# Gated attention and a low-rank mixer on one core: the mixer's work in three places per batch instead of four

## The chip, the cores and the metric

The kernel runs on one core of a Trainium2 chip. Its time is the device time of one execution in microseconds (us). TensorE (PE) multiplies, ScalarE (ACT) and VectorE (DVE) work on the results, GpSimd (POOL) issues most of the transfers and SyncE (SP) issues the transposing ones. Each engine works through its own queue in the order in which the program wrote it, and waits at an instruction until its semaphores are there.

## The reference

Two blocks, one behind the other, for 8 batches of 3136 positions with 256 channels (z has 64):

```python
scores = (1.0 / S) * np.matmul(z, z.transpose(0, 2, 1))
attn = np.maximum(scores, 0.0) ** 2
x = u * np.matmul(attn, v)                 # gated attention

h = x.transpose(0, 2, 1) @ U @ V           # U: 3136 x 32, V: 32 x 3136
y = x + h.transpose(0, 2, 1)               # low-rank mixing of the positions
out = y + np.maximum(y @ w_ch1, 0.0) @ w_ch2   # 256 -> 1024 -> 256
```

The low-rank sums `x^T U` need all positions of a batch; so the second block of a batch can only start when its attention is done.

## The kernel before, in words

**Tiles.** A batch has 25 tiles of 128 positions, the last with 64 (`NF`). An "output" is one such tile of the attention's result. The outputs of a batch are made in the order 12, 13, ..., 24, 0, ..., 11; the loop counts them as i = 0 to 24 (`turns(i)`), and this text says "output i" with that count. Two outputs share a pair of PSUM banks (a "pair": 0 and 1, 2 and 3, ..., 10 and 11; output 12, the short tile, stands alone; then 13 and 14, and so on).

**Attention.** z is laid twice, on both halves of the 128 partitions, so that two matmuls of 64 rows run side by side in the array. The score matrix is symmetric, so `A[j]` holds 13 blocks of a row of tiles (`score`, L307 on TensorE, relu on ACT L320, square on DVE L322), and the other 12 blocks of an output come as a "strip": a DMA transpose of `A` (`turn`, L342) that SP issues four outputs ahead. Output i multiplies its 25 blocks with v (`half`, L420; `quarter`, L460, for the short tile). When a pair is complete, `close_pair` adds the two banks (ACT L434, DVE L435), multiplies with u and writes x (DVE L450). A pair that opens takes the set of banks that the pair before it did not use; the other set is the `spare()` one.

**Mixer.** The 25 outputs of a batch form seven chunks of 4, 4, 4, 3, 4, 4 and 2. `rank_once` (L534) makes the rank sums with 25 matmuls of 128 x 32; `low_rank` (matmuls L586, adds on DVE L600) adds the low-rank part to a chunk of x in place and has it transposed (`turn_x`, L559, SP). `up_steps` (L618, relu on ACT L636) and `down_steps` (L665) are the two layers. A down step of a pair ends in an add on DVE (L679) into one of two `o_sb` buffers and in a store that POOL issues (L692; L694 for the short tile). `low_rank` and the down steps use the spare banks.

**The order of the work is written by hand.** While batch b's attention runs, the mixer of batch b-1 is done in between. Behind output 0 come the rank sums of b-1. `ahead` puts `low_rank` of chunks 0 to 6 inside outputs 2, 3, 6, 7, 10, 11 and 14, at step 10, 12 or 17 of the 25. `bursts_of(b)` makes a list of eight mixer steps: step n is the up layer of chunk n merged with the down layer of chunk n-1 (step 0 has only up, step 7 only down). `burst_at` places them, two and two, behind outputs 4, 8, 13 and 17. The scores that later outputs and the next batch need are spread into the outputs (`own_at`, `next_at`, `_spread`). The next batch's v comes in nine loads (`V_PARTS`, L244 and L247), merged into the mixer steps; its z is loaded at output 1 (output 5 in batch 1), copied twice on DVE (`double_z`, L188) in a mixer step, and transposed by SP at outputs 7 and 10 (`turn_z`, L195). In the last batch the steps of chunk 6 wait in `late`, and behind the loop stands the mixer of the last batch.

**Where x lies.** `x_bf` has room for 32 tiles, as eight slots of four. Chunk c of batch b takes slot (7 b + c) mod 8. The weights `w_ch1` pass through slots 6 and 7 at the start.

Of the kernel before, what the change touches and what calls it, by code (L numbers as in the profile page):

```python
# [8 lines left out]
BF16 = mybir.dt.bfloat16  # L9
# [5 lines left out]
def _ceil_div(a, b):  # L15
    return (a + b - 1) // b
# [26 lines left out]
def kernel(  # L43
# [28 lines left out]
    FIRST = HALF  # L72
# [1 line left out]
    LEAD = FIRST + AHEAD  # L74
    NG = 4
    XR = 32
    XB = 28

    ctx.enter_context(
        tc.manual_schedule(engines={ENG.PE, ENG.SP, ENG.Pool, ENG.DVE, ENG.Activation})  # L80
# [1 line left out]
    persist = ctx.enter_context(tc.tile_pool(name="persist", bufs=1))  # L82
# [42 lines left out]

    v_both = [persist.tile([P, NT, D], BF16, name=f"v{k}") for k in range(2)]
    eye = persist.tile([P, P], BF16, name="eye")
    x_bf = persist.tile([P, XR // 4, 4 * D], BF16, name="x_bf")
    A = [persist.tile([P, NB * P], BF16, name=f"A{j}") for j in range(NT)]


# [3 lines left out]
    def place(t):  # L135
        return (t - FIRST) % NT
# [9 lines left out]
    chunks = [[0, 1, 2, 3], [4, 5, 6, 7], [8, 9, 10, 11], [12, 13, 14]]  # L146
    chunks += [[15, 16, 17, 18], [19, 20, 21, 22], [23, 24]]
    chunks = [[turns(i) for i in c] for c in chunks]
    widths = [sum(P if t < NF else TAIL for t in c) for c in chunks]
    NC = len(chunks)  # L150
    offset = {t: (n, k) for n, c in enumerate(chunks) for k, t in enumerate(c)}

    def group(b, c):
        n = len(chunks[c])
        flat = x_bf[:, ((XB // 4) * b + c) % (XR // 4), : n * D]
        return flat.rearrange("p (a t c) -> p a t c", a=ND, c=P)

    def x_at(b, t, n=1):
# [81 lines left out]
    def load_v(b, part):  # L240
        t0, t1 = part
        v_bf = v_both[b % 2]
        if t0 < NF:
            pool_dma(out=v_bf[:, t0:t1, :], in_=rows(v[b])[:, t0:t1, :])  # L244
        else:
            for r in halves:
                pool_dma(out=v_bf[r, NF, :], in_=v[b, NF * P :, :])  # L247

    V_PARTS = [(t, t + 3) for t in range(0, NF, 3)] + [(NF, NT)]
    WHOLE = ((0, NF),)  # L250

    def weight_steps():


        w1_tmp = x_bf[:, NC - 1 :, :].rearrange("p a h -> p (a h)")
        w1_tmp = w1_tmp[:, : ND * H].rearrange("p (a h) -> p a h", a=ND)

        def first_w():
            pool_dma(out=w1_tmp, in_=moe_w_ch1.rearrange("(t p) d -> p t d", p=P))

        def second_w():
            pool_dma(out=w2_bf, in_=moe_w_ch2.rearrange("(p t) d -> p t d", t=NH))

        def order_w(a):
            nc.vector.tensor_copy(
                out=w1_bf[:, a, :].rearrange("p (t q) -> p t q", q=P),
                in_=w1_tmp[:, a, :].rearrange("p (q t) -> p t q", t=NH),
            )
# [26 lines left out]
        orders = [lambda a=a: order_w(a) for a in range(ND)]  # L295
        return fetches, second_w, puts + [put_tail, copies] + orders
# [403 lines left out]
    def bursts_of(b):  # L700

        out_ = []
        for c in range(NC + 1):
            alone = c == 0 or (c == NC - 1 and b == B - 2)
            up = [lambda s=s, c=c, a=alone: up_steps(c, a)[s]() for s in range(NH // 2)]
            up = up if c < NC else []
            down = down_steps(b, c - 1) if c else []
            out_.append((up, down))
        return out_
# [183 lines left out]
    start_up()  # L893
    puts = dict(zip((13, 14, 15, 16, 17, 18, 19, 20), puts))
    late = []
    for b in range(B):
        more = b + 1 < B
        begin = 0 if b else 2 * NG
        bursts = bursts_of(b - 1) if b else []
        burst_at = {4: (0, 1), 8: (2, 3), 13: (4, 5), 17: (6, 7)}  # L900
        own = own_at if b else first_at
        v_at = dict(zip((14, 16, 18, 20, 22, 10), V_PARTS[3:]))
        ahead = dict(zip((2, 3, 6, 7, 10, 11, 14), range(NC)))
        for i in range(begin, NT):
            o = turns(i)
            fill = [s for key in own.get(i, ()) for s in score_steps(b, *key)]
            if b == 0 and i in first_new:
                fill += rebuild_steps(b, first_new[i])
            if b == 0 and i in first_more:
                fill.append(lambda pair=first_more[i]: make_stored(pair, LEAD + 2 * NG))  # L910
            if more:
                coming = next_at if b else after_first
                fill += [s for key in coming[i] for s in score_steps(b + 1, *key)]
                if b and i == (1 if b > 1 else 5):
                    load_z(b + 1, WHOLE)
                if b == 0 and i == 9:
                    double_z(b + 1, ((FIRST, NF), (0, FIRST)))
                if i == (7 if b > 1 else 11 - 2 * b):
                    turn_z(b + 1, ((FIRST, NF),))
                if i == (10 if b else 12):  # L920
                    turn_z(b + 1, ((0, FIRST),))
                if b == 0 and i in v_at:
                    load_v(b + 1, v_at[i])
                if i == (12 if b else 14):
                    extend_z(b + 1)
            main = attend_steps(b, o)
            if b and i in ahead:
                at = 17 if (i + (i > FIRST)) % 2 == 0 else 12 if i == 7 else 10
                main.insert(at, lambda c=ahead[i]: low_rank(b - 1, c))
            _spread(main, fill)  # L930
            if b == 0 and i in first_turns:
                for t in first_turns[i]:
                    turn(b, t)
            elif i + AHEAD < NT:
                turn(b, turns(i + AHEAD))
            elif more:
                turn(b + 1, turns(i + AHEAD - NT))
            elif i == NT - AHEAD:
                turn_x(b, 0)
            if b == 0 and i in puts:  # L940
                puts[i]()
            if (b, i) == ((1, 1) if more or b else (0, 20)):
                second_w()
            if b and i == 0:
                rank_once(b - 1, spare()[0])
            for n in burst_at.get(i, ()) if b else ():
                up, down = bursts[n]
                if not more and n >= NC - 1:
                    late += up + (down if n == NC else [])
                    up, down = [], (down if n < NC else [])  # L950

                steps = [down.pop(0)] if n == 4 else []
                steps += _merge(up, down)
                if more:
                    loads = [lambda k=k: load_v(b + 1, V_PARTS[k]) for k in ((n,) if n < NC else (n, n + 1))]
                    steps = _merge(steps, loads)
                    if n == (1 if b > 1 else 3):
                        for k, part in ((6, (FIRST, NF)), (3, (0, FIRST))):
                            steps.insert(k, lambda part=part: double_z(b + 1, (part,)))
                run(steps)  # L960
# [4 lines left out]
    b = B - 1  # L965
    last = bursts_of(b)
# [9 lines left out]
    for c in range(NC + 1):  # L976
        up, down = last[c]
        steps = _merge(up, down)
# [32 lines left out]
```

## Time and profile before

| | us |
|---|---|
| runs | 999.24, 994.98, 994.67 |
| median | 994.98 |
| profiled execution | 1000.6 |
| its span, first to last instruction | 998.9 |
| TensorE busy in it | 983.7 |
| ScalarE, VectorE, GpSimd busy | 614.8, 554.7, 170.3 |
| rank sums of batches 1 to 7 start at | 101.2, 222.95, 348.6, 469.58, 590.56, 713.58, 834.56 |

The page gives busy times by engine and by line. An answer by windows gives, for a stretch of the span, its length, the busy time of PE, PEld, DVE, ACT and POOL with the number of instructions, the granted TensorE clock (1.00 is full), the share of the DMA engines and GB/s. A line of the timeline has the start, the length, engine, line, operation, tiles (written<-read), the shape of the array and of the operand, and how many; a bracket holds the idle time before it and what ended it. Starts are measured; the end of a matmul is modelled, so neighbouring lines overlap. A line of waits has the waiting group, the group waited for, the sum in us, the number of times and the longest.

### The profile page before, as it was taken

To read this page: it belongs to the slowest core of one execution; us is meant where nothing else is said; L and a number is where in the kernel's file an instruction comes from. 1 tells how busy PE (TensorE), PEld (TensorE's weight loads), DVE (VectorE), ACT (ScalarE), POOL (GpSimd) and SP (SyncE) were. 2 spreads that over 40 slices of the span, in tenths; PEclk is the share of its full clock that TensorE was granted. 3 is DMA by queue.
4 is the path that set the end of the run, shared out by engine and by line. 5 is a ranking of instruction groups with operands and counts; after the bars stand their busy time and mean duration, and the time that the engine had idled before them with its cause. 6 is when DMAs were issued, how large, how long until landed. Compare 5 with 4: busy or idle time off the path is not lost.

```text
span 998.9 us, 31057 instructions
## 1 busy us (share of the span) xinstructions
PE 983.7 (98%) x13697; PEld 780.3 (78%) x13697; DVE 554.7 (56%) x1020; ACT 614.8 (62%) x845; POOL 170.3 (17%) x316
## 2 busy tenths in 40 slices
PE   8999999999998999999999999999999999999998
PEld 5778777887877878788787887778878788787866
DVE  6888654466544665456644566445664457542352
ACT  8978764577644776466754667556674666643154
POOL 5111112211111111221112211112111120011000
PEclk9999999999999999999999999999999999999999
DMA  9999989899899998999899997999979997679633
GB/s 197 167 181 196 196 161 203 174 171 170 168 165 165 172 170 173 180 177 172 158 178 178 182 168 148 187 167 182 170 149 194 173 185 157 124 149 163 129 93 104
DMA packets 410728, 167.17 MB, mean 167 GB/s; under 512 B 386320, under 2 KB 395216, under 8 KB 410592
## 3 DMA queue, kind: packets, MB, share of 16 engines
q1 hardware_dynamic: 382272, 98.90, 62.8%
q0 software_dynamic: 28320, 66.28, 28.8%
q8 instruction: 107, 1.75, 0.8%
q14 instruction: 29, 0.24, 0.1%
HBM read 61.88 MB, written 25.69 MB: 88 GB/s over the span
## 4 chain that ended last, share of the span: by engine, by line
PE 88%; DMA 5%; issue 3%; DVE 2%; ACT 1%; POOL 1%; DVEq 0%; POOLq 0%; ACTq 0%
PE ps L420 47%; PE ps L665 16%; PE ps L618 16%; PE ps L307 7%; DMA out_dram<-o_sb 3%; DMA strip<-A 1%; PE ps L586 1%; ACT A L320 1%; PE ps L460 1%; DVE A L322 1%; DMA zT<-z_bf 1%; PE ps L534 1%; DMA ut<-x_bf 1%; DVE both L435 0%; PE ps L207 0%
## 5 line engine op out<-in xcount | busy, mean ns | idle before, releaser
L320 ACT ACTIVATE A<-ps 128x832 bf16<-128x832 f32 (+9 forms) x481 | 359.2, 764 | 150.1 <-PE ps L307 143.9
L420 PE MATMUL ps<-v,A 64*128 64x256 bf16 x4988 | 342.3, 270 | 2.3 <-DVE A L322 1.1
L322 DVE TENSOR_TENSOR A<-A 128x832 bf16<-128x832 bf16 (+9 forms) x481 | 243.9, 523 | 127.3 <-ACT A L320 125.5
L420 PE MATMUL ps<-v,strip 64*128 64x256 bf16 x4420 | 308.2, 269 | 1.4 <-DMA strip<-A 1.4
L420 PEld LDWEIGHTS <-A 64*128 64x128 bf16 x4988 | 248.3, 94 | 45.3 <-issue 10.5
L636 ACT ACTIVATE relu_bf<-ps 128x1024 bf16<-128x1024 f32 (+2 forms) x206 | 186.3, 912 | 140.2 <-PE ps L618 140.2
L420 PEld LDWEIGHTS <-strip 64*128 64x128 bf16 x4420 | 224.8, 94 | 34.2 <-DMA strip<-A 2.3
L679 DVE TENSOR_TENSOR o_sb<-ps,x_bf 128x512 f32<-128x512 f32 (+2 forms) x105 | 69.9, 665 | 244.4 <-PE ps L665 214.2
L665 PE MATMUL ps<-w_bf,relu_bf 128*128 128x256 bf16 (+1 forms) x1600 | 201.2, 273 | 0.0
L618 PE MATMUL ps<-ut,w_bf 128*128 128x512 bf16 (+2 forms) x896 | 198.6, 353 | 0.4 <-DMA ut<-x_bf 0.4
L665 PEld LDWEIGHTS <-relu_bf 128*128 128x128 bf16 (+1 forms) x1600 | 152.9, 98 | 45.6 <-issue 3.6
L618 PEld LDWEIGHTS <-w_bf 128*128 128x128 bf16 x896 | 84.9, 98 | 62.5 <-issue 6.5
L404 POOL DMA_DIRECT2D u_sb<-in_u_dram x96 | 53.7, 560 | 462.9 <-DVE x_bf L450 440.6
L307 PE MATMUL ps<-zT 64*128 64x416 bf16 (+9 forms) x812 | 132.3, 313 | 0.1
L434 ACT COPY both<-ps 128x512 f32<-128x512 f32 (+1 forms) x104 | 58.9, 567 | 73.2 <-PE ps L420 67.1
L692 POOL DMA_DIRECT2D out_dram<-o_sb x84 | 45.9, 547 | 276.2 <-DVE o_sb L679 269.8
L435 DVE TENSOR_TENSOR both<-ps,both 128x512 f32<-128x512 f32 (+1 forms) x104 | 69.3, 666 | 28.6 <-ACT both L434 28.0
L600 DVE TENSOR_TENSOR x_bf<-ps,x_bf 128x512 bf16<-128x512 f32 (+1 forms) x112 | 65.5, 626 | 11.6 <-PE ps L586 11.3
L450 DVE TENSOR_TENSOR x_bf<-both,u_sb 128x512 bf16<-128x512 f32 (+1 forms) x104 | 69.8, 671 | 3.6
L307 PEld LDWEIGHTS <-zT 64*128 64x128 bf16 x812 | 43.5, 94 | 4.2 <-DMA zT<-z_bf 0.4
L244 POOL DMA_DIRECT2D v<-in_v_dram x61 | 34.1, 561 | 1.2 <-DMA z_c<-in_z_dram 0.8
L307 PE MATMUL ps<-relu_bf 64*128 64x416 bf16 (+9 forms) x117 | 23.1, 337 | 3.1 <-ACT A L320 2.2
(61 smaller groups left out, 212.9 us busy)
## 6 DMA issues: line engine op xcount, KB each, us to landing
u_sb<-in_u_dram POOLq DMA_DIRECT2D x96, 256.0 KB, 3.8
out_dram<-o_sb POOLq DMA_DIRECT2D x84, 256.0 KB, 3.3
v<-in_v_dram POOLq DMA_DIRECT2D x57, 192.0 KB, 4.7
strip<-A SPq DMA_TRANSPOSE x194, 5.4
out_dram<-o_sb SPq DMA_DIRECT2D x11, 256.0 KB, 2.0
z_c<-in_z_dram POOLq DMA_DIRECT2D x7, 384.0 KB, 5.9
u_sb<-in_u_dram POOLq DMA_DIRECT2D x16, 64.0 KB, 2.7
ut<-x_bf SPq DMA_TRANSPOSE x56, 3.7
```

The lines of the kernel that those rows point to most:

```text
L307: mm(out=ps[:, k, :n], lhsT=zT[halves[k], j, :], rhs=zT_flat[halves[k], c : c + n], start=True, stop=True,)
L320: nc.scalar.activation(out=dst, in_=src, func=AF.Relu, scale=sc)
L322: nc.vector.tensor_tensor(out=dst, in0=dst, in1=dst, op=ALU.mult)
L420: mm(out=acc[t0][h][:, (o - t0) * D : (o - t0 + 1) * D], lhsT=w[halves[h]], rhs=v_both[b % 2][halves[h], j, :], start=start, stop=stop, **kw,)
L434: nc.scalar.copy(out=both[:, :w], in_=banks[1][:, :w])
L435: nc.vector.tensor_tensor(out=both[:, :w], in0=banks[0][:, :w], in1=both[:, :w], op=ALU.add)
L450: nc.vector.tensor_tensor(out=x_at(b, t0, n), in0=split(both[:, :w]), in1=u_sb[:, :n, :].rearrange("p t (a c) -> p t a c", c=P), op=ALU.mult,)
L600: nc.vector.tensor_tensor(out=q, in0=split(ps[h][:, : len(ks) * D]), in1=q, op=ALU.add)
L618: mm(out=ps[i][:, :w] if apart else ps[:, i, :w], lhsT=w1_bf[:, db, (hp + i) * P : (hp + i + 1) * P], rhs=uT[c][:, db, len(chunks[c]) * P ...
L636: nc.scalar.activation(out=relus[c][:, hp : hp + 2, :w], in_=ps[:, :, :w], func=AF.Relu)
L665: mm(out=ps[r, k * D : (k + 1) * D], lhsT=relus[c][:, ht, q : q + (TAIL if two else P)], rhs=w2_bf[:, ht, :], start=(ht < 1 + two), stop=( ...
L679: nc.vector.tensor_tensor(out=o_sb[:p].rearrange("p t (a c) -> p t a c", c=P), in0=split(ps[:p, k0 * D : (k + 1) * D]), in1=x_at(b, t, nk) ...
```

## The change

The mixer steps of a batch are placed three times instead of four: steps 0, 1, 2 behind output 4, steps 3, 4, 5 behind output 10, and steps 6, 7 behind output 0 of the batch after the next, directly behind the rank sums of the next one. (The last batch keeps steps 6 and 7 of the batch before it behind output 17, as it was.) Batch 1 has no place behind output 0. `low_rank` moves to outputs 1, 2, 3, 6, 7, 9 and 14. The down sums of the short tile no longer open their place; they lie inside the run of three. Chunks 5 and 6 of x now live into the batch after the next, so the slots of four are gone: `place_groups` lists for each chunk when it is first written and last read, and finds each a place among the 32 tiles. v's nine loads go one into each mixer step, and what is left of them (one, or three in batch 1) to outputs 13, 15 and 17. In batch 1 z's copies stand at output 8, outside a mixer step.

```diff
-    XB = 28
...
+    def bursts_at(b):
+
+        at = {0: (NC - 1, NC)} if b > 1 else {}
+        if b:
+            at.update({4: (0, 1, 2), 10: (3, 4, 5)})
+        if b == B - 1:
+            at[17] = (NC - 1, NC)
+        return at
+
+    def place_groups():
+
+        items = []
+        for b in range(B):
+            for c, ts in enumerate(chunks):
+                begin = b * NT + place(ts[0]) + (0 if place(ts[0]) == FIRST else 1)
+                last = NT * B
+                for d in (1, 2):
+                    for i, ns in bursts_at(b + d).items() if b + d < B else ():
+                        if c + 1 in ns and (d == 1) == (i > 0) and not (b == B - 2 and c == NC - 1):
+                            last = (b + d) * NT + i
+                items.append((begin, last, len(ts), (b, c)))
+        items.sort()
...
+        return {items[k][3]: p for k, p in enumerate(at)}
+
+    spot = place_groups()
+
     def group(b, c):
         n = len(chunks[c])
-        flat = x_bf[:, ((XB // 4) * b + c) % (XR // 4), : n * D]
+        flat = x_bf[:, spot[b, c] * D : (spot[b, c] + n) * D]
...
-        bursts = bursts_of(b - 1) if b else []
-        burst_at = {4: (0, 1), 8: (2, 3), 13: (4, 5), 17: (6, 7)}
+        all_bursts.append(bursts_of(b))
+        burst_at = bursts_at(b)
+        v_in = list(V_PARTS) if more and b else []
...
-        ahead = dict(zip((2, 3, 6, 7, 10, 11, 14), range(NC)))
+        ahead = dict(zip((1, 2, 3, 6, 7, 9, 14), range(NC)))
...
-                if b == 0 and i == 9:
+                if b < 2 and i == (8 if b else 9):
                     double_z(b + 1, ((FIRST, NF), (0, FIRST)))
...
+                if i in (13, 15, 17) and v_in:
+                    load_v(b + 1, v_in.pop(0))
...
-            for n in burst_at.get(i, ()) if b else ():
-                up, down = bursts[n]
-                if not more and n >= NC - 1:
+            for n in burst_at.get(i, ()):
+                up, down = all_bursts[b - 1 if i else b - 2][n]
+                if i and not more and n >= NC - 1:
                     late += up + (down if n == NC else [])
                     up, down = [], (down if n < NC else [])
 
-                steps = [down.pop(0)] if n == 4 else []
+                steps = [down.pop(0)] if n == 4 and n == burst_at[i][0] else []
                 steps += _merge(up, down)
                 if more:
-                    loads = [lambda k=k: load_v(b + 1, V_PARTS[k]) for k in ((n,) if n < NC else (n, n + 1))]
-                    steps = _merge(steps, loads)
-                    if n == (1 if b > 1 else 3):
+                    steps = _merge(steps, [lambda part=part: load_v(b + 1, part) for part in [v_in.pop(0)]])
+                    if b > 1 and n == 1:
                         for k, part in ((6, (FIRST, NF)), (3, (0, FIRST))):
                             steps.insert(k, lambda part=part: double_z(b + 1, (part,)))
                 run(steps)
```

More of the change, by code (lines that the diff above doesn't have):

```diff
@@ L127 @@
     eye = persist.tile([P, P], BF16, name="eye")
-    x_bf = persist.tile([P, XR // 4, 4 * D], BF16, name="x_bf")
+    x_bf = persist.tile([P, XR * D], BF16, name="x_bf")
     A = [persist.tile([P, NB * P], BF16, name=f"A{j}") for j in range(NT)]
@@ L151, with put_in @@
     offset = {t: (n, k) for n, c in enumerate(chunks) for k, t in enumerate(c)}
+    def bursts_at(b):
[17 more added lines that the diff above has]
+        items.sort()
+        at = []
+        def put_in(k):
+            if k == len(items):
+                return True
+            begin, last, n, _ = items[k]
+            held = [
+                (at[m], at[m] + items[m][2]) for m in range(k) if items[m][1] >= begin
+            ]
+            for p in sorted({0} | {q1 for _, q1 in held} | {q0 - n for q0, _ in held}):
+                if 0 <= p <= XR - n and all(p + n <= q0 or q1 <= p for q0, q1 in held):
+                    at.append(p)
+                    if put_in(k + 1):
+                        return True
+                    at.pop()
+            return False
+        assert put_in(0)
+        return {items[k][3]: p for k, p in enumerate(at)}
+    spot = place_groups()
     def group(b, c):
         n = len(chunks[c])
-        flat = x_bf[:, ((XB // 4) * b + c) % (XR // 4), : n * D]
+        flat = x_bf[:, spot[b, c] * D : (spot[b, c] + n) * D]
         return flat.rearrange("p (a t c) -> p a t c", a=ND, c=P)
@@ L252, in weight_steps @@
     def weight_steps():
-        w1_tmp = x_bf[:, NC - 1 :, :].rearrange("p a h -> p (a h)")
-        w1_tmp = w1_tmp[:, : ND * H].rearrange("p (a h) -> p a h", a=ND)
+        w1_tmp = x_bf[:, (NT - 1) * D : (NT - 1) * D + ND * H].rearrange("p (a h) -> p a h", a=ND)
         def first_w():
@@ L895 @@
     late = []
+    all_bursts = []
     for b in range(B):
```

## The prediction

> **What bounds the kernel now.** I read the page's busy table, then the stages of one batch each, then who waited for whom, then the timeline around mixer places. "Output i" is the i-th attention output of a batch in loop order (0 to 24), a "place" a run of mixer steps behind an output.
>
> The busy table, and the same table cut at the rank sums (L534) of batches 1 to 7, one line per batch:
>
> ```profile
> PE 983.7 (98%) x13697; PEld 780.3 (78%) x13697; DVE 554.7 (56%) x1020; ACT 614.8 (62%) x845; POOL 170.3 (17%) x316
> ...
> 101.20:222.95 121.75, 121.22 (x1706) 96.32 (x1704) 67.07 (x122) 75.50 (x103) 22.46 (x42) 1.00 0.96 180
> 222.95:348.60 125.65, 122.83 (x1707) 98.67 (x1705) 67.14 (x122) 75.59 (x103) 21.76 (x41) 0.99 0.98 168
> 348.60:469.58 120.98, 120.98 (x1705) 96.39 (x1703) 67.08 (x122) 75.60 (x103) 21.73 (x41) 1.00 0.97 175
> 469.58:590.56 120.98, 120.98 (x1705) 96.39 (x1703) 66.98 (x122) 75.50 (x103) 21.73 (x41) 1.00 0.97 173
> 590.56:713.58 123.02, 121.35 (x1706) 98.17 (x1704) 66.69 (x122) 75.52 (x103) 21.73 (x41) 1.00 0.97 172
> 713.58:834.56 120.98, 120.98 (x1705) 96.39 (x1703) 67.08 (x122) 75.61 (x103) 21.75 (x41) 1.00 0.96 174
> ```
>
> TensorE is the bound. Three batches take 120.98 us to the hundredth, busy throughout: nothing else shows in them. The others take 0.77, 4.67 and 2.04 us more, 7.5 us together. The profiled execution took 1000.6 us (span 998.9 and 1.7 around it); without the 7.5 it would be 993.1. The median, 994.98, so still has about 1.9 us of such waits.
>
> Where they come from, in the waits (us in total, times, longest) and the chain behind the longest:
>
> ```profile
> DVE o_sb L679 <- DMA out_dram<-o_sb: 30.0, 8, 5.5
> ...
> PE ps L586 <- DVE o_sb L679: 3.5, 2, 2.8
> ...
> PE ps L420 <- DVE o_sb L679: 1.0, 1, 1.0
> ```
>
> ```profile
> 292.87 10.01 DMA out_dram<-o_sb
> ...
> 303.00 0.70 DVE o_sb L679
> 303.75 0.29 PE ps L586 x2
> ```
>
> There are two o_sb buffers, so the add of an output pair waits for the store of the pair two before it. Behind the place at output 13 a store took 10.01 us, the add sat on DVE, and `low_rank` at output 14, which needs the PSUM banks that this add reads, held TensorE. It happened again at 670.39. The third (1.0 us, at about 643) is the next pair's opening behind the place at output 8.
>
> What entering and leaving a place costs, on TensorE's timeline (start, length):
>
> ```profile
> 409.50 0.94 PE L420 MATMUL ps<-v,A 64*128 64x256 bf16 x14
> 410.27 0.19 PE L307 MATMUL ps<-zT 64*128 64x64 bf16 x2
> ...
> 412.21 0.27 PE L420 MATMUL ps<-v,A 64*128 64x256 bf16 x2
> 412.42 0.63 PE L665 MATMUL ps<-w_bf,relu_bf 128*64 128x256 bf16 x8
> ...
> 424.26 1.04 PE L665 MATMUL ps<-w_bf,relu_bf 128*128 128x256 bf16 x8
> 425.23 0.72 PE L420 MATMUL ps<-v,A 64*128 64x256 bf16 x10
> ```
>
> Seven pairs of half-array matmuls start in 0.77 us, 0.11 a pair; the last pair before L665 takes 0.21. Eight L665 matmuls take 0.87 (8 x 0.109, as everywhere in these runs of steps), yet L420 starts 0.97 after them. Each change of array shape (64\*128, 128\*128, 128\*64, 128\*32) costs 0.10 us.
>
> **The change, part by part.**
>
> *Shape changes.* Counted in the two built orders of matmuls: 121 before, 108 after, on the same 13697 matmuls. In a batch from 2 to 6: four places made 8, rank sums 2, output 12 (64\*64) 2, and one more because the place at 13 opened with the 128\*64 sums of the short tile: 13. After: 128\*32 goes straight into the mixer, so rank sums and place 0 make 3; two places 4; the 128\*64 sums now lie inside a place, 2; output 12 2: 11. That is 10 fewer over five batches, 3 fewer in batch 1 (no place at 0), none in batch 7. 13 x 0.10 = 1.3 us less, all on TensorE's path. The Trainium skill, "TensorEngine Tiling (Array Packing)", Key Properties, says that changing the tiling mode, not merely the tile, drains TensorE; it gives no time.
>
> *Places 13 and 17 go.* With 13 goes the wait of `low_rank` at output 14: the nearest place is then three outputs (some 8 us) back. In the profile these waits were worth 2.98 us (303.75 less 300.22 and five pairs) and 0.7 us idle and, behind the first, a slow clock:
>
> ```profile
> 303.70:307.30 3.60, 3.56 (x44) 3.04 (x45) 2.00 (x5) 2.15 (x3) 0.54 (x1) 0.69 0.39 110
> ```
>
> Granted clock 0.69; that batch's 4.67 is thus 2.98 idle and about 1.6 of slow clock. Together 5.3 us off the profile, and batch 1's 0.77 (a chunk transpose late for its place at 8, z's late at output 12) too, since both now have a place more of lead.
>
> *The place at 10 is three steps.* It stores six times (one of them the short tile). From steps in the trace (L665 x8 0.87, L618 x4 0.87 at 512 columns, 0.55 at 320): pairs end 2.8, 5.7, 7.2, 10.6, 15.0 and 18.5 us in. A store is issued 1.2 us after its pair ends (0.7 of it the add) and lands a median 3.3 later. The third add wants the first store at 7.2 against 2.8+1.2+3.3 = 7.3: DVE waits, TensorE not, because the bank of that add is next written at about 12.4. The first store may be some 8 us late before TensorE stops. The place at 4 stores four times, 3.5 us apart, and needs nothing new.
>
> *The place at 0.* It is the old place 17 moved: up of chunk 6, down of 5 and 6, three stores. But `low_rank` of chunk 0 now follows at output 1, step 10:
>
> ```profile
> 437.69 0.61 PE L618 MATMUL ps<-ut,w_bf 128*128 128x256 bf16 x4
> ...
> 444.78 0.39 PE L420 MATMUL ps<-v,A 64*128 64x256 bf16 x4
> ```
>
> ```profile
> 441.50 0.55 POOL L692 DMA_DIRECT2D out_dram<-o_sb  x1 [3.27 <-DVE o_sb L679]
> ...
> 444.88 0.69 DVE L679 TENSOR_TENSOR o_sb<-ps,x_bf 128x512 f32<-128x512 f32 x1 [1.05 <-PE ps L665]
> ```
>
> On this pattern the third add ends 445.57 and `low_rank` would come at 444.78+1.27 = 446.05 (ten steps and a score, as 355.88 to 357.15 in batch 3): 0.5 us to spare. The first store must land by 446.05-0.69-0.05 = 445.3, that is within 3.8 us. Medians at place 17 are 2.8 to 4.1, so I take 0.1 us a batch (0.6), with 0 below and, at 6.3, the median of the short tile's store (behind output 13), 2.5 us a batch above. The Trainium skill, "DMA: Bandwidth & Descriptors", Anatomy of one DMA, fits 2.0 us plus bytes over 436 kB per us: an estimate of 2.6 for 256 KB, by which this wait never comes; the trace's median is 3.3.
>
> *`low_rank` moves* from outputs 2,3,6,7,10,11,14 to 1,2,3,6,7,9,14. Its matmuls and adds are the same. At an odd output its DVE adds (2 x 0.69) must end before the next pair opens on those banks. Behind output 3 that costs: 359.34 x10 takes 0.66 to the next group where 355.88 x10 takes 0.55. So 0.11 more behind outputs 1 and 9, 14 times: 0 (as behind output 7: 383.18 to 383.73, 0.55) to 1.5; I take 0.7.
>
> *v and z.* v's nine loads a batch (0.55 us of POOL each, no wait but on a buffer freed a batch ago) go two at place 0, three at 4, three at 10, one at 13: done earlier, so nothing waits. They stand between stores, as before. In batch 1 z's four copies (0.35 and 0.58 us, 1.85 together) move to output 8's start on DVE, between scores; ACT, not DVE, frees score banks, so 0 for TensorE, at most 0.5 once. SP keeps its order except that chunk transposes go with `low_rank`; each is earlier than its place needs it. Outputs 11 to 24 now run without a place; strips there were issued 13 us ahead and landed in 4 to 8, so no cost.
>
> *x by lifetime.* Chunks 5 and 6 of x live on to the next batch's place 0. New x is written by DVE behind the adds that read the old: no new wait across engines, 0.
>
> Sum: 1000.6 - 5.3 - 0.8 - 1.3 + 0.6 + 0.7 = 994.5 against the profile, which keeps the 1.2 us wait of batch 5 at 643. Against the median: 994.98 - 1.3 + 0.6 + 0.7 less half of its 1.9 us of waits = 994.0. Ends: with no waits and none added, 993.1 - 1.3 = 991.8. I predict 994.0.
>
> **Rivals.**
>
> *The mixer waits for its stores (slower).* At place 0 every first store takes 6.3 us: six batches x 2.5 = 15 us, and 1009 us; from 4.7 us on (0.9 x 6 = 5.4) it passes +0.5%. For: stores of 4 to 10 us at outputs 8 to 13, and u, strip and v transfers that run beside. Against: place 17 had the same neighbours, and took 2.8 to 4.1. Behind the 2.98 us wait the clock fell, behind the 0.7 and 1.2 us ones (batch 5: 1.00) it did not. The Trainium skill, "TensorE: Matmul & The Clock Gate", Part 1, has the clock halved after an idle window of about 3.4 us, so that by it only the longest of these stalls would cost more than itself.
>
> *The crowding moves.* Long transfers (285 to 303 and 634 to 670) hit wherever they fall, stores of the six-pair place among them; half of the profile's waits stay: 993.1 - 1.3 + 1.3 + 3.7 = 996.8, to 999.9.
>
> *Faster by over 0.5%.* Below 990.0 needs 2 us beyond the clean 991.8; nothing in the trace offers it.
>
> *Strips starve* in the fourteen outputs without a place: needs landings of over 13 us; the worst seen is 12.1, among stores. Price: 1 us each, 7 and more in all.
>
> **How the numbers follow.** Forecast (991.8 to 996.5) 0.70; stores 0.16, half of it over +5 us; crowding 0.10; faster 0.03; strips 0.01. About 5 us, 0.5%, is what a measurement here can tell from no change. Faster 0.03; slower 0.08 + 0.01 = 0.09; same 0.88. The range 991.6 to 999.0 leaves the far half of the stores' case and a little below.
>
> **What would show it.** Clean batches of 120.98 - 0.2 + up to 0.3; no wait of L420 or of `low_rank` behind output 13; 0.10 us at fewer shape changes. Wrong if `low_rank` at output 1 waits for DVE's output add by over 0.9 us in every batch, or if strips or A hold TensorE between outputs 11 and 24.

## The result, and the profile after

The changed kernel takes 1031.99 us, median of 6 runs (1022.90 to 1035.18), beside 997.19 us (6 runs, 994.67 to 1008.68) for the kernel before: a ratio of 1.0317, 95% interval 1.0254 to 1.038. It is slower by 3.2%, and far outside the predicted range of 991.6 to 999.0. The profiled execution of it took 1022.9 us (span 1021.2) and is the quickest of the six; what the other five lost beyond it is not in a trace. Here and below, a ratio leaves out single executions that took over 1.5% more than the fastest of the same kernel (one of e3's, one of e5's, one of the kernel before beside e1 to e4), while medians and ranges keep them.

In the changed kernel the lines have moved: the attention's matmuls are L462 (were L420), scores L349, up L660, down L707, `low_rank` L628 with its adds on DVE L642, `turn` L384, `turn_x` L601, the output add L721, the scores' relu L362 and square L364, `turn_z` L238.

The page of the changed kernel, busy times, then the shares of the chain that ended last, then one group:

```profile
PE 988.9 (97%) x13657; PEld 792.1 (78%) x13697; DVE 553.7 (54%) x1020; ACT 616.4 (60%) x845; POOL 170.1 (17%) x316
...
PE 87%; DMA 8%; DVE 3%; ACT 2%; issue 1%; DVEq 0%
...
L462 PE MATMUL ps<-v,strip 64*128 64x256 bf16 x4420 | 311.5, 269 | 18.7 <-DMA strip<-A 18.7
```

TensorE is busy for 5 us more (a slower clock), and 8% of the chain that sets the end is now one kind of transfer: the strips. (40 matmul records of L660 are missing from this trace, so small gaps among them are not lost time.) The waits say the same, and say what is not there: no line of `low_rank` waiting for an output add is left.

```profile
DVE o_sb L721 <- DMA out_dram<-o_sb: 25.8, 11, 4.6
...
PE ps L462 <- DMA strip<-A: 18.7, 11, 5.3
...
PE ps L462 <- DVE x_bf L642: 2.3, 7, 0.3
```

By windows, cut at the rank sums of batches 1 to 7, and below them short stretches behind single waits (columns as before; the one behind the busy times is the granted clock):

```profile
100.95:216.39 115.44, 114.21 (x1636) 91.94 (x1639) 64.71 (x119) 73.36 (x99) 20.57 (x39) 1.00 0.99 183
216.39:338.64 122.25, 121.26 (x1700) 98.20 (x1704) 66.84 (x122) 75.75 (x103) 21.73 (x41) 1.00 0.92 171
338.64:470.40 131.76, 123.76 (x1700) 98.81 (x1703) 66.85 (x122) 75.86 (x103) 21.73 (x41) 0.97 0.91 161
470.40:602.01 131.61, 124.25 (x1700) 99.50 (x1703) 66.84 (x122) 75.75 (x103) 21.74 (x41) 0.97 0.92 161
602.01:724.71 122.70, 121.26 (x1700) 98.23 (x1704) 66.84 (x122) 75.75 (x103) 21.33 (x40) 1.00 0.92 172
724.71:848.27 123.56, 121.25 (x1701) 98.22 (x1704) 66.86 (x122) 75.75 (x103) 22.19 (x41) 1.00 0.92 170
...
366.20:369.80 3.60, 3.38 (x8) 1.29 (x10) 0.49 (x1) 1.02 (x1) 0.00 (x0) 0.50 1.19 258
...
407.40:411.00 3.60, 3.60 (x30) 2.84 (x31) 0.36 (x1) 1.41 (x2) 0.00 (x0) 1.00 1.25 261
```

No batch is clean any more. (Batch 1 is shorter because its steps 6 and 7 now stand in batch 2; the tail behind 848.27 is longer by about as much.) Batches 3 and 4 take 8 to 9.5 us more than batches 2, 5 and 6. TensorE's timeline in batch 3 shows where:

```profile
360.31 0.60 PE L462 MATMUL ps<-v,strip 64*128 64x256 bf16 x7
366.20 0.39 PE L462 MATMUL ps<-v,strip 64*128 64x256 bf16 x1 [5.30 <-DMA strip<-A]
...
404.05 1.47 PE L462 MATMUL ps<-v,strip 64*128 64x256 bf16 x23
407.38 0.28 PE L462 MATMUL ps<-v,strip 64*128 64x256 bf16 x1 [1.86 <-DMA strip<-A]
```

Each time it is one matmul, the last of output 4 and the last of output 10, directly ahead of the runs of three. That matmul takes the short tile's block, and for an even output up to output 10 this block lies in the strip of the next one: the last matmul of output 4 reads strip 5, the last of output 10 reads strip 11. So these strips are wanted one output earlier than their number says, and for strip 11 no place lies between issue and use any more. Behind 5.30 us without work the clock is 0.50 for 3.6 us, behind 1.86 us it stays at 1.00.

SP's timeline in batch 3, before and then after (start, length of the issue):

```profile
348.69 1.42 SPq L342 DMA_TRANSPOSE strip<-A  x1
357.27 1.23 SPq L559 DMA_TRANSPOSE ut<-x_bf  x1
...
388.15 9.60 SPq L342 DMA_TRANSPOSE strip<-A  x3
```

```profile
335.67 1.43 SPq L384 DMA_TRANSPOSE strip<-A  x1
350.48 1.50 SPq L601 DMA_TRANSPOSE ut<-x_bf  x1
352.07 6.74 SPq L384 DMA_TRANSPOSE strip<-A  x1
358.87 6.09 SPq L601 DMA_TRANSPOSE ut<-x_bf  x1
...
396.99 3.31 SPq L238 DMA_TRANSPOSE zT<-z_bf  x1
400.40 1.26 SPq L601 DMA_TRANSPOSE ut<-x_bf  x1
401.77 3.43 SPq L384 DMA_TRANSPOSE strip<-A  x2
```

Before, SP issued strip 5 (348.69) as soon as the rank sums began. After, chunk 0's transpose stands ahead of it and waits for the second add of `low_rank` in output 1: SP issues nothing from 337.1 to 350.48, place 0 passes meanwhile, and strip 5 follows at 352.07. Strip 11 (before, the first of the three at 388.15) now leaves SP at 401.77, behind z's transpose and chunk 4's. Its matmul starts 5.6 us later, at 407.38, and has then waited 1.9 of them.

For every batch, from SP's issue, the landing in the record of the transfer and the start of the first matmul that reads it (us, batches 1 to 7):

| | issued ahead of the need | landing took |
|---|---|---|
| strip 5, before | 14.0 each | 7.7 7.2 5.8 7.5 7.8 9.0 4.7 |
| strip 5, after | 8.8 to 8.9 (14.1, 11.9 where the matmul waited for it) | 5.6 6.5 14.1 11.8 8.6 8.8 6.0 |
| strip 11, before | 15.1 to 18.7 | 4.7 3.8 7.3 4.3 3.8 6.7 5.3 |
| strip 11, after | 4.9 to 7.6, as long as the landing: the matmul waits each time. Without the wait 3.4 to 5.5 | 6.2 4.9 5.6 7.5 5.1 5.4 6.2 |

The theory to be tested: (a) all of the loss but some 5 us is strips 5 and 11 landing late; (b) strip 5 by SP's order and by the crowd of transfers at output 1; (c) strip 11 because the place at output 8 is gone. Rivals: the run of three itself is slow, through u, x or stores; or the openings behind the moved `low_rank` are what costs.

### The profile page after: what moved, and what is told of

Read it like the earlier page. It is cut to its first block, busy times and chain, and to the rows that moved or that the text cites. A ratio compares the mean times of both kernels' runs of the same rounds, so it can differ in the third digit from the quotient of the medians.

```text
span 1021.2 us, 31029 instructions
## 1 busy us (share of the span) xinstructions
PE 988.9 (97%) x13657; PEld 792.1 (78%) x13697; DVE 553.7 (54%) x1020; ACT 616.4 (60%) x845; POOL 170.1 (17%) x316
## 4 chain that ended last, share of the span: by engine, by line
PE 87%; DMA 8%; DVE 3%; ACT 2%; issue 1%; DVEq 0%
PE ps L462 43%; PE ps L707 17%; PE ps L660 17%; DMA strip<-A 8%; PE ps L349 6%; ACT A L362 2%; DVE x_bf L642 1%; PE ps L502 1%; DVE A L364 1%; PE ps L628 1%; PE ps L576 1%; PE ps L250 0%; PE ps L266 0%; PE ps L559 0%; DVE both L477 0%
## 5 line engine op out<-in xcount | busy, mean ns | idle before, releaser
L362 ACT ACTIVATE A<-ps 128x832 bf16<-128x832 f32 (+9 forms) x481 | 359.5, 764 | 155.6 <-PE ps L349 150.3
L462 PE MATMUL ps<-v,A 64*128 64x256 bf16 x4988 | 348.2, 269 | 4.1 <-DVE x_bf L642 2.3
L462 PE MATMUL ps<-v,strip 64*128 64x256 bf16 x4420 | 311.5, 269 | 18.7 <-DMA strip<-A 18.7
L364 DVE TENSOR_TENSOR A<-A 128x832 bf16<-128x832 bf16 (+9 forms) x481 | 244.3, 523 | 130.4 <-ACT A L362 127.2
L462 PEld LDWEIGHTS <-A 64*128 64x128 bf16 x4988 | 259.8, 94 | 44.7 <-issue 13.9
L462 PEld LDWEIGHTS <-strip 64*128 64x128 bf16 x4420 | 233.2, 94 | 50.7 <-DMA strip<-A 21.8
L721 DVE TENSOR_TENSOR o_sb<-ps,x_bf 128x512 f32<-128x512 f32 (+2 forms) x105 | 69.9, 666 | 248.6 <-PE ps L707 205.2
L707 PE MATMUL ps<-w_bf,relu_bf 128*128 128x256 bf16 (+1 forms) x1600 | 202.9, 274 | 0.4
L660 PE MATMUL ps<-ut,w_bf 128*128 128x512 bf16 (+2 forms) x856 | 199.6, 356 | 1.9 <-issue 0.2
L707 PEld LDWEIGHTS <-relu_bf 128*128 128x128 bf16 (+1 forms) x1600 | 153.8, 99 | 48.4 <-issue 5.5
L349 PE MATMUL ps<-zT 64*128 64x416 bf16 (+9 forms) x812 | 139.4, 312 | 0.0
L660 PEld LDWEIGHTS <-w_bf 128*128 128x128 bf16 x896 | 85.9, 99 | 62.2 <-issue 8.6
L642 DVE TENSOR_TENSOR x_bf<-ps,x_bf 128x512 bf16<-128x512 f32 (+1 forms) x112 | 65.4, 626 | 6.2 <-PE ps L628 6.1
L349 PEld LDWEIGHTS <-zT 64*128 64x128 bf16 x812 | 50.7, 94 | 3.3
L349 PE MATMUL ps<-relu_bf 64*128 64x416 bf16 (+9 forms) x117 | 23.1, 337 | 2.8 <-ACT A L362 2.2
```

The lines of the kernel that those rows point to most:

```text
L349: mm(out=ps[:, k, :n], lhsT=zT[halves[k], j, :], rhs=zT_flat[halves[k], c : c + n], start=True, stop=True,)
L362: nc.scalar.activation(out=dst, in_=src, func=AF.Relu, scale=sc)
L364: nc.vector.tensor_tensor(out=dst, in0=dst, in1=dst, op=ALU.mult)
L462: mm(out=acc[t0][h][:, (o - t0) * D : (o - t0 + 1) * D], lhsT=w[halves[h]], rhs=v_both[b % 2][halves[h], j, :], start=start, stop=stop, **kw,)
L642: nc.vector.tensor_tensor(out=q, in0=split(ps[h][:, : len(ks) * D]), in1=q, op=ALU.add)
L660: mm(out=ps[i][:, :w] if apart else ps[:, i, :w], lhsT=w1_bf[:, db, (hp + i) * P : (hp + i + 1) * P], rhs=uT[c][:, db, len(chunks[c]) * P ...
```

## The experiments

Each edit is on the changed kernel unless said. `load_z`, `turn` and the rest are the kernel's own names. Each ratio is against the kernel before on the same chip.

**e1_strip5, e2_strip11, e3_both: the order in SP's queue.** Strip 5 is issued at the start of output 1 (e1), strip 11 at the start of output 7 (e2), or both (e3).

```diff
+            early = b > 0 and i in (1,)          # (7,), (1, 7)
+            if early:
+                turn(b, turns(i + AHEAD))
...
-                turn(b, turns(i + AHEAD))
+                if not early:
+                    turn(b, turns(i + AHEAD))
```

> The changed kernel, with one transpose moved in SP's queue: the strip of output 5 is put at the start of output 1, in front of chunk 0's transpose, instead of at its end, behind it. Theory Q (queue order on SP): in the profile of the changed kernel this strip is issued 8.9 to 13.3 us before its first use at the end of output 4, where before it had 14; with the move it is issued at the end of output 0, over 20 us ahead, the waits at the end of output 4 (8.4 us, and about 3 of slow clock behind the longest) go, and those at the end of output 10 (10.7 us and 2.6 of clock) stay. Expected 1010 to 1022 us. Rival C (the transfers are crowded, whatever the order): the strips go on landing 9 to 14 us after issue and some other strip or chunk transpose is late in its place; 1025 to 1032. Rival P (the new openings behind low_rank at output 1, about 0.6 us a batch, and DVE's waits for stores are what costs): no change, 1028 to 1034.

> The changed kernel, with the strip of output 11 put at the start of output 7, in front of z's transpose and of chunk 4's, instead of at its end. Theory Q: it was issued 5 to 7.5 us before its first use at the end of output 10, and lands in 5 to 7.5; with the move it is issued some 4 us earlier, so the waits at output 10 (0.5 to 4.1 us a batch, 10.7 in all, and slow clock behind the longest) go; those at output 4 stay. Expected 1015 to 1024 us. Rival C: only part of it goes, because the transpose is then among z's and chunk 3's and lands later: 1024 to 1032. Rival P: no change, 1028 to 1034.

> Both moves of the two runs before. Theory Q: no wait of a strip use is left in batches 1 to 7, a batch takes 121.5 us or less, and the time is that of the kernel before within 4 us: 994 to 1001, the rest above it being the openings behind low_rank at output 1. Rival C: waits remain for strips that come later in the queue: 1010 to 1025. Rival P: 1028 to 1034.

Measured: e1 1012.68 us (1008.32 to 1013.82, 4 runs), ratio 1.0169 (1.0135 to 1.0204). Strip 5 goes out 22 us ahead (14.5 in batch 1), and no matmul waits at output 4; the seven waits at output 10 stay (0.2 to 5.2 us). e2 1018.77 us (1016.12 to 1019.81), ratio 1.0235 (1.0205 to 1.0264): strip 11 is 8 us ahead and waits in batch 4 alone (1.7 us); four waits at output 4 stay (5.2, 3.1, 2.9, 1.8 us). e3 1003.96 us (1001.18 to 1020.43, 5 runs), ratio 1.0085 (1.0054 to 1.0117), and no matmul waits for strip 5 or, but for 0.1 us in batch 4, for strip 11. Two of e3's batches by windows, and its waits:

```profile
215.84:337.58 121.74, 121.33 (x1706) 98.18 (x1705) 66.84 (x122) 75.69 (x103) 21.80 (x41) 1.00 0.95 172
337.58:463.43 125.85, 122.94 (x1705) 98.56 (x1703) 66.83 (x122) 75.79 (x103) 21.75 (x41) 0.99 0.93 168
```

```profile
PE ps L660 <- DMA ut<-x_bf: 2.5, 1, 2.5
PE ps L462 <- DVE x_bf L642: 2.3, 7, 0.3
...
PE ps L462 <- DMA strip<-A: 1.0, 2, 0.6
```

By the ratios, each against the kernel before on its own chip, the excess falls from 3.17% to 0.85%: the two strips are some 23 of 32 us (19.6 us between the spans of the two profiled executions, 1021.2 and 1001.6). What is left is clean batches of 121.73 against 120.98 before, and a transposed x that came 2.5 us late once (chunk 0's, which now stands behind the strip), with a slower clock behind it. So (a) holds in the main, but some 8.5 us are left and not 5: e3's median lies above the 994 to 1001 that the theory gave it.

**e4_z_earlier, e11_place17, e9_ahead234: what makes strip 5 late.** e4 leaves SP's order and takes z's load away from output 1; e11 puts steps 6 and 7 back behind output 17; e9 moves `low_rank` of the first three chunks one output on, so that strip 5 stands ahead of chunk 0.

```diff
# e4_z_earlier
-                if b and i == (1 if b > 1 else 5):
+                if b == 1 and i == 5:
                     load_z(b + 1, WHOLE)
+                if b and i == 20 and b + 2 < B:
+                    load_z(b + 2, WHOLE)
# e11_place17
-        at = {0: (NC - 1, NC)} if b > 1 else {}
-        if b:
-            at.update({4: (0, 1, 2), 10: (3, 4, 5)})
-        if b == B - 1:
-            at[17] = (NC - 1, NC)
-        return at
+        if not b:
+            return {}
+        return {4: (0, 1, 2), 10: (3, 4, 5), 17: (NC - 1, NC)}
...
-                if i in (13, 15, 17) and v_in:
+                if i == 13 and v_in:
# e9_ahead234
-        ahead = dict(zip((1, 2, 3, 6, 7, 9, 14), range(NC)))
+        ahead = dict(zip((2, 3, 4, 6, 7, 9, 14), range(NC)))
```

> The changed kernel, with the load of the next z (three transfers, 400 KB) taken from output 1, where it runs beside the late strip of output 5, to output 20 of the batch before; SP's order is left as the change made it. Theory Q: the strip of output 5 is still issued about 9 us ahead; its landing time falls from 9 to 14 towards 6 us, so most of the waits at output 4 go, but not those at output 10: 1015 to 1026 us. Rival C in its strong form (crowding alone, at both places): both kinds of waits shrink by over half, below 1015. Rival P: no change.

> The changed kernel with the place of steps 6 and 7 back behind output 17 of the same batch, as in the kernel before; the runs of three behind outputs 4 and 10, the outputs of low_rank and SP's order at output 1 stay as changed. Theory (strip 5, late behind chunk 0, also has to land among place 0's stores and v loads): strip 5 is still issued 8.9 us ahead but lands in 5 to 8, so no wait at output 4; the waits at output 10 stay at 0.2 to 4 us; batches of 122 to 126 us and 1003 to 1013 us. Rival (place 0 has no part in it, z's load and SP's order are enough): strip 5 lands in 8.9 us and more in some batches as in the changed kernel, waits of 2 to 5 us at output 4 stay, and the time is 1015 us or more.

> The changed kernel, with low_rank of chunks 0, 1 and 2 at outputs 2, 3 and 4 instead of 1, 2 and 3. SP then meets the strip of output 5 before chunk 0's transpose, without any move of the strip. Theory Q: the waits at output 4 go and those at output 10 stay, and the opening at output 2 costs nothing: 1005 to 1016 us, a little better than with that strip moved (1012.7). Rival C: the crowd is the same (z, u, three chunk transposes), so the waits stay in part: 1018 and more. A risk of its own: chunk 2's transpose may be late for its step of the place at 4.

Measured: e4 1011.31 us (1008.21 to 1013.31), ratio 1.0161 (1.0129 to 1.0193); e11 1014.61 us (1010.94 to 1015.45), ratio 1.0179 (1.0137 to 1.0222); e9 1006.31 us (1002.69 to 1010.10), ratio 1.0111 (1.0071 to 1.0151); 4 runs each. In all three no matmul in batches 1 to 7 waits for strip 5. In e4 and e11 it is still issued 8.6 to 8.9 us ahead, but lands in 5.1 to 8.2 and in 5.5 to 7.0 us instead of 5.6 to 14.1. In e9 it is issued some 21 us ahead, the opening behind output 1 costs nothing, and the waits at output 10 stay (0.3 to 1.9 us); one wait of 1.4 us for a transposed x, at the place of output 4 in batch 3, is new. Two totals missed the theory. e4's is under its 1015 to 1026, where the rival of crowding at both places had put it; but that rival asked for both kinds of waits to shrink by over half, and those at output 10 stay (0.2 to 4.1 us). e11's is over its 1013: its profiled execution reached the first rank sums only at 107.4 (100.95 in the changed kernel), behind a wait of 3.9 us for a strip of batch 0 and a granted clock of 0.51 over the next 6 us, ahead of the places that were edited.

What crowds in is seen in the changed kernel's DMA issues in 350.0 to 366.2 (batch 3; KB each, median us to landing):

```profile
z_c<-in_z_dram POOLq DMA_DIRECT2D x1, 384.0 KB, 8.4
...
v<-in_v_dram POOLq DMA_DIRECT2D x1, 192.0 KB, 7.8
ut<-x_bf SPq DMA_TRANSPOSE x2, 11.8
z_c<-in_z_dram POOLq DMA_DIRECT2D x2, 8.0 KB, 10.5
strip<-A SPq DMA_TRANSPOSE x2, 9.7
```

With z gone from there (e4, the matching stretch, 353.4 to 367.0), strips take a median 7.1:

```profile
strip<-A SPq DMA_TRANSPOSE x4, 7.1
```

So (b) is three things together at output 1: SP's order takes 5 us of lead (14.0 to 8.9), z's load and place 0's stores and v loads lengthen the landing, and with any one of the three away the strip is in time. Where all three are left as they are, it is late again: in e2 and in e5 (below) strip 5 holds the matmul in four of the seven batches, by 1.8 to 6.2 us, with landings of 10.7 to 14.8. Stores and v loads were not taken apart. The Trainium skill, "DMA: Bandwidth & Descriptors", Issuing engines are not separate DMA queues, says that transfers issued by different engines share the same 16 DMA engines and interleave. e4 agrees: moving a load that POOL issues took the strip that SP issues in batch 3 from 14.1 to 8.2 us (batches 2 to 6: 6.5 to 14.1 with z beside it, 5.1 to 8.2 without).

**e5_place8: what makes strip 11 late.** The second run of three stands behind output 8, and chunk 5's `low_rank` in output 8.

```diff
-            at.update({4: (0, 1, 2), 10: (3, 4, 5)})
+            at.update({4: (0, 1, 2), 8: (3, 4, 5)})
...
-        ahead = dict(zip((1, 2, 3, 6, 7, 9, 14), range(NC)))
+        ahead = dict(zip((1, 2, 3, 6, 7, 8, 14), range(NC)))
```

> The changed kernel, with its second place two outputs earlier, behind output 8 instead of 10 (steps 3, 4, 5 as before; low_rank of chunk 5 goes to output 8 to be ready). SP's queue keeps its order. Theory Q: the strip of output 11 is wanted at the end of output 10; it came too late because the place that stood behind output 8 (some 11 us) is gone between its issue and its use. With a place there again it lands some 15 us before its use: the waits at output 10 go, those at output 4 stay: 1015 to 1024 us, as with that strip moved forward (1018.8). Rival C (crowded transfers): the strip's issue and landing are as late relative to its outputs, and the waits stay in part: 1024 to 1032.

Measured: 1019.58 us (1012.26 to 1031.33, 4 runs), ratio 1.0192 (1.0142 to 1.0243). Strip 11 goes out 22 to 26 us ahead and never waits; the five strip waits that are left are at output 4 and at the start:

```profile
PE ps L462 <- DMA strip<-A: 14.5, 5, 6.0
PE ps L707 <- DVE x_bf L642: 3.0, 7, 1.4
```

So (c) holds: a run of mixer steps between a strip's issue and its use is what had covered it. The second line is new, some 0.4 us a batch: down steps behind the adds of chunk 5's `low_rank`, which now stands directly ahead of the place.

**e7_before_ahead: the moved `low_rank` alone, on the kernel before.**

```diff
-        ahead = dict(zip((2, 3, 6, 7, 10, 11, 14), range(NC)))
+        ahead = dict(zip((1, 2, 3, 6, 7, 9, 14), range(NC)))
```

> The kernel before, with one part of the change alone: low_rank at outputs 1, 2, 3, 6, 7, 9 and 14 instead of 2, 3, 6, 7, 10, 11 and 14; places, x, v and z as before. Theory Q: chunk 0's transpose now stands before the strip of output 5 in SP's queue also here; that strip is issued about 9 us before its use instead of 14, so some batches wait at output 4; output 11's strip has a place in between and does not. With the openings (0.5 us a batch) 998 to 1012 us. Rival: the queue order only hurts with the new places: within 2 us of before plus the openings, 996 to 1000.

Measured: 1007.58 us (1006.10 to 1009.75, 4 runs), ratio 1.0125 (1.0093 to 1.0156). Strip 5 is issued 8.9 us ahead here too, and lands in 5.5 to 7.5: no wait at output 4, where the theory had expected some. Strip 11, with the place at 8 still there, is 15 to 19 us ahead. It is slower all the same, for openings and for z's transposes that came late at outputs 12 and 13:

```profile
PE ps L307 <- DMA zT<-z_bf: 4.0, 4, 1.6
...
PE ps L420 <- DVE x_bf L600: 2.3, 7, 0.3
```

The late zT is this hybrid's own (the changed kernel has no such wait); the openings are in both. Its quietest batch takes 122.26 us, 1.28 over the kernel before, more than the 0.85 that the openings come to in e3 (below); the rest was not traced.

**e6_both_step4, e8_best, e10_three: what is left.** e6 is e3 with `low_rank` of outputs 1 and 9 at step 4 instead of 10. e8 adds e4's z. e10 has `low_rank` at outputs 2, 3, 4, 6, 7, 9 (step 4) and 14, strip 11 issued early, and e4's z.

```diff
# e6_both_step4, e8_best
-                at = 17 if (i + (i > FIRST)) % 2 == 0 else 12 if i == 7 else 10
+                at = 17 if (i + (i > FIRST)) % 2 == 0 else 12 if i == 7 else 4 if i in (1, 9) else 10
# e10_three
-        ahead = dict(zip((1, 2, 3, 6, 7, 9, 14), range(NC)))
+        ahead = dict(zip((2, 3, 4, 6, 7, 9, 14), range(NC)))
...
+            early = b > 0 and i in (7,)
...
+                at = 17 if (i + (i > FIRST)) % 2 == 0 else 12 if i == 7 else 4 if i == 9 else 10
```

> Both strips moved forward (1003.96 us), and low_rank at outputs 1 and 9 put at step 4 instead of step 10 of the output. Theory O: what is left over the kernel before is, batch by batch, the opening of the next pair, which waits until DVE has added the low-rank part out of those banks (at output 2 0.58 us, at output 10 some 0.17), because DVE works off a score's square first; six steps earlier the adds are done in time. Expected a clean batch of 121.1 us instead of 121.73 and 999 to 1001 us. Rival: the openings are not what costs, or the low-rank matmuls then wait themselves for the banks: 1003 to 1006.

> The changed kernel with four things put right at once: strips 5 and 11 are issued at the start of outputs 1 and 7, low_rank at outputs 1 and 9 stands at step 4, and z is loaded at output 20 of the batch before. Theory (the strips are all that was lost, beside half a microsecond per opening): no wait on a strip, a clean batch of 121.2 to 121.4 us and 994 to 999 us. Rival (the place of three steps itself costs, through u or the stores that come late in it): batches of 122 us and more and over 1002 us.

> The changed kernel with low_rank at outputs 2, 3, 4, 6, 7, 9 and 14 (that of output 9 at step 4), strip 11 issued at the start of output 7, and z loaded at output 20 of the batch before. Chunk 0's transpose then stands behind strip 5 by the loop's own order. Theory: no wait on a strip and no late opening at output 2; a clean batch of 120.8 to 121.1 us and 990 to 996 us, level with the kernel before or up to 0.5% under it, since 11 shape changes a batch take 0.2 us less than 13. Rival (the chunk of output 4 is transposed too near its place): a wait of L660 on the transposed x behind output 4 of 0.5 us and more per batch, and 998 us or more.

Measured: e6 1000.01 us (996.59 to 1011.10, 10 runs), ratio 1.0062 (1.0025 to 1.01); its profiled execution has one wait of 4.6 us in batch 4, scores behind ACT, which itself stood 6.0 us behind a strip's transfer. Its clean batch fell by about half of what was expected (to 121.38, not 121.1). e8 998.87 us (996.35 to 1007.26, 12 runs), ratio 1.0034 (1.0004 to 1.0063). e10 995.32 us (993.53 to 1001.17, 12 runs), ratio 1.0007 (0.9992 to 1.0023). The clean batch goes from 121.73 (e3) to 121.38 (e6, e8) and 121.09 (e10), whose batches 2 to 6 are all alike:

```profile
217.57:338.66 121.09, 121.09 (x1705) 97.33 (x1703) 66.62 (x122) 75.70 (x103) 21.77 (x41) 1.00 0.97 179
338.66:459.76 121.10, 121.09 (x1706) 97.33 (x1705) 66.62 (x122) 75.73 (x103) 21.75 (x41) 1.00 0.98 171
459.76:580.90 121.14, 121.14 (x1706) 97.32 (x1705) 66.53 (x122) 75.72 (x103) 21.79 (x41) 1.00 0.98 178
580.90:701.99 121.09, 121.08 (x1706) 97.33 (x1704) 66.63 (x122) 75.71 (x103) 21.79 (x41) 1.00 0.95 175
701.99:823.08 121.09, 121.08 (x1705) 97.34 (x1703) 66.62 (x122) 75.71 (x103) 20.15 (x38) 1.00 0.93 170
```

e10 has the three places, the x groups by lifetime, the runs of three and the new spread of v: all of it together costs nothing that these runs can tell (0.07%, -0.08 to 0.23) once the strips are in time and the openings shorter. It does not beat the kernel before either; no run here does.

## Why the prediction was wrong, point by point

**The step that failed** is "SP keeps its order except that chunk transposes go with `low_rank`; each is earlier than its place needs it. Outputs 11 to 24 now run without a place; strips there were issued 13 us ahead and landed in 4 to 8, so no cost." It asked of the moved transpose whether it comes in time itself, not what stands behind it in SP's queue while it waits for DVE. And it looked for outputs without a place in 11 to 24 only, where strips do hold; the stretch from output 5 to 10 lost its place too. What the runs showed in its stead: strips 5 and 11 late, some 23 of the 32 us by the ratios of the changed kernel and of e3. In the profiled execution the nine waits are 19.1 us (5.5 and 2.9 at output 4; 0.7, 0.5, 2.0, 4.1, 0.9, 1.8, 0.7 at output 10; each as the delay against the usual spacing of the matmuls). Batches 3 and 4 lost another 2.6 and 2.9 us to the clock: 131.76 and 131.61 less e3's clean 121.73 less their waits of 7.48 and 7.02. The clock's own rows behind the two longest waits, 0.50 and 0.78 in batch 3 and 0.50 and 0.66 in batch 4 over 3.6 us each, come to 2.6 and 3.0. Together 24.5. With some 5 for the openings (6, less 1 for shape changes) and the 7.5 of waits that the profile of before had and this one has not, that is 24.5 + 5 - 7.5 = 22.0 of the 22.3 us by which the span grew.

**The rival "strips starve"** named the transfer but not the mechanism: it asked for landings of over 13 us against a lead of 13. The lead fell instead. For strip 11, with 3.4 to 5.5 us, ordinary landings of 4.9 to 7.5 were late; for strip 5, with 8.9, it still took landings of 11.8 and 14.1, in the crowd at output 1. Its 1 us each was 0.5 to 5.5. It got 0.01, and the sign of being wrong that went with it, strips holding TensorE between outputs 11 and 24, did not come. (The longest landing in the profile before is 12.3; the 12.1 is a median of two.)

**The openings** were mis-sized. Forecast: 0.11 behind outputs 1 and 9, 0.7 us in all, at most 1.5. Measured on e3's clean batch, against the gaps of the clean batch before (0.29 us in all): 1.14 us, so 0.85 more a batch, 0.58 of it at the opening of output 2 alone. Over seven batches that is 6 us. In the row chosen (359.34, behind output 3) squares of scores stood ahead of the adds as well, but the adds began 1.07 us behind the first matmul of `low_rank` (357.15 to 358.22) and the pair opened 2.19 us behind it. At output 1 a square waits for ACT, and these are 1.28 and 2.02 us. DVE and TensorE there, in the changed kernel:

```profile
347.88 0.38 PE L628 MATMUL ps<-t_sb,V_bf 64*128 64x256 bf16 x4
...
348.65 0.59 DVE L364 TENSOR_TENSOR A<-A 128x832 bf16<-128x832 bf16 x1 [1.25 <-ACT A L362]
...
349.16 1.28 DVE L642 TENSOR_TENSOR x_bf<-ps,x_bf 128x512 bf16<-128x512 f32 x2
...
350.50 0.70 PE L462 MATMUL ps<-v,A 64*128 64x256 bf16 x9 [0.33 <-DVE x_bf L642]
```

`low_rank`'s matmuls are through at 348.3, but its adds start at 349.16, behind a square that itself waited 1.25 us for ACT; the second add ends at 350.44, and the pair that opens, from 349.90 on, waits. At step 4 (e6, e8) this wait is gone, and 0.29 us appears inside `low_rank` instead; at output 2 (e9, e10) it costs nothing.

**Shape changes.** Forecast: 11 instead of 13, 0.20 us a batch less. e10's clean batch less its gaps is 121.09 - 0.54 = 120.55, that of the kernel before 120.98 - 0.29 = 120.69: 0.14 less. Right in sign, and two thirds of the size.

**The waits of `low_rank` behind the place at 13** went as forecast; no wait of `low_rank` for an output add is left in any version with the runs of three. But of the 7.5 us that the profile of before lost, most had been that execution's own: its median had about 2.

**The stores.** In the run of six pairs DVE waits and TensorE does not, as worked out, in the changed kernel and in e10 (121.09 to 121.14 in five batches); e3, e6 and e8 have single waits of 0.4 to 1.3 us for an output add. At place 0, 0.6 us was taken for the first store; it landed in 2.3 to 3.4 us in all six batches, within the 3.8, and nothing waited. The rival of the waiting stores falls with that. So does "the crowding moves" as it was put: not the stores lengthened (a median of 2.5 us, before 3.3), but the strips beside them.

**x by lifetime and v** were costed at nothing, and e10 bears that out within its interval. z's load stayed at output 1 and was not costed; e4 shows that it was one of the three causes at output 4.

## What to carry to other kernels

Before moving an instruction that waits, list what stands behind it in the same queue, and give each of these its own lead: time from issue to first reader, less the longest landing seen. Removing a stretch of other work costs every transfer whose lead ran through it, ahead of the new place as well as behind it; and the first reader may be another loop step than the name says, so look it up in the order of the instructions.

## What the runs showed that was not expected

How long a wait has to be before the clock falls is not fixed. In the changed kernel it fell behind 5.30 us idle (the window at 366.20) and behind 3.92 us in batch 4, and stayed at 1.00 behind 1.86 and 2.77 us. But it fell behind shorter waits elsewhere: to 0.69 in the kernel before (the 2.98 us of the prediction, 2.82 of them idle), to 0.55 in e3 behind 2.50 us and to 0.53 in e5 behind 2.08 us. The changed kernel's batches 3 and 4, then e3 and e5:

```profile
369.80:373.40 3.60, 3.60 (x14) 1.47 (x13) 1.43 (x4) 2.11 (x3) 0.00 (x0) 0.78 1.20 239
...
536.00:539.60 3.60, 3.41 (x15) 2.13 (x16) 0.00 (x0) 0.70 (x1) 0.00 (x0) 0.50 1.13 217
539.60:543.20 3.60, 3.60 (x22) 2.56 (x21) 0.69 (x1) 1.06 (x2) 0.00 (x0) 0.66 1.15 211
```

```profile
362.40:366.00 3.60, 3.58 (x10) 1.35 (x11) 0.69 (x1) 1.05 (x2) 0.00 (x0) 0.55 1.19 240
```

```profile
746.50:750.10 3.60, 3.55 (x9) 1.29 (x10) 0.54 (x1) 1.02 (x1) 0.00 (x0) 0.53 1.21 289
```

The Trainium skill, "TensorE: Matmul & The Clock Gate", Part 1, has the clock halved after an idle window of about 3.4 us. The waits of 5.30 and 3.92 us agree; those of 2.08 to 2.82 us, behind which it fell, do not, and what sets them apart from the 2.77 us without a fall is not shown here. In the changed kernel each of the two falls cost 2.6 to 3.0 us more than the wait itself.

The length of a transposing issue on SP is not fixed. In the changed kernel the issue of a strip takes 1.3 to 6.7 us, a median of 1.7; the two longest transposing issues, 6.74 and 6.09, stand in the crowded stretch from 352 to 365. There they held up the transposes that had not been issued yet; that the crowd made them long was not tested.
